# Two of four mean subtractions in each layer norm given to GpSimd, with a third difference buffer

## The chip, the cores and the metric

The kernel runs on one core of a Trainium2 chip. A core has five engines with queues of their own: TensorE (PE in the profile: matmuls, and PEld for its weight loads), VectorE (DVE), ScalarE (ACT), GpSimd (POOL) and SyncE (SP, which here only starts DMAs). Every engine works through its queue strictly in order and waits on semaphores for the others. The metric is the time of one execution on the device in microseconds (us).

## The reference

The input x has 2048 rows of 1024 features, in bfloat16. Four blocks follow one another, A, B, A, B, each with a residual:

```python
def _layernorm(x, axis=-1, eps=1e-5):
    m = jnp.mean(x, axis=axis, keepdims=True)
    v = jnp.var(x, axis=axis, keepdims=True)
    return (x - m) / jnp.sqrt(v + eps)
...
x = x + _A_ref(_layernorm(x, axis=-1), A_wqkv, A_w_phi, A_wo)
x = x + _B_ref(_layernorm(x, axis=-1), B_wqkv, B_wo)
x = x + _A_ref(_layernorm(x, axis=-1), A_wqkv, A_w_phi, A_wo)
x = x + _B_ref(_layernorm(x, axis=-1), B_wqkv, B_wo)
```

A is linear attention with 32 heads of 32: queries and keys go through a small projection w_phi, and two softmaxes over 32 features (of the value and of its negative) make the feature maps. B is softmax attention with 32 heads over all 2048 rows. The change touches only the subtraction x - m.

## The kernel before

The residual x stays in SBUF, transposed: xT has the 1024 features as 8 groups of 128 partitions, and the 2048 rows lie along the free dimension, in four chunks c of 512. A "layer" is one A block with the B block after it. In layer 0, A's keys and values are made chunk by chunk (`a_keys`, L651), then the queries and the output of A chunk by chunk (`a_queries`, `a_out`), and behind each chunk the layer norm of B for it, then B's keys and values; after that comes B's attention. Its scores are matmuls at L1049, three 128x512 blocks to one exponential on ScalarE (L1095); a number of the blocks go to VectorE instead (L1171 and L1013). The sums over keys are the matmuls of L1199. While layer 0's attention runs, its layer norms and keys for layer 1's A block are made beside it for three of the chunks (`alone=True`). Layer 1 makes those of the fourth chunk by itself, then goes on as layer 0 does.

`layernorm` (L524) for one chunk:
- squares of x on ScalarE (L536; on VectorE at L541 when alone), and two groups of eight matmuls with a matrix of 1/1024 (through `mmgroup`, recorded at L480) that give mean and mean square in every partition
- mean squared and a copy of the mean to SBUF on ScalarE (L556, L558); the variance on VectorE (L559, one input in PSUM, one in SBUF); log and exponential on ScalarE (L561, L563) give the reciprocal deviation
- for i = 0 to 3, each two feature groups, 128 x 1024 elements: the subtraction s_i (L569: x in bfloat16 minus the mean, into a float32 buffer of the class "lnw") and the multiplication m_i (L573: that buffer times the reciprocal deviation, into bfloat16). The matmuls of keys, queries or values take the four parts one after the other.

There are 16 such layer norms: three are alone, inside the attention of layer 0, and 13 are not: 4 for A and 4 for B in layer 0, 1 for A and 4 for B in layer 1. I call them A0 to A3 and B0 to B3 by their chunk.

The order on every engine is made by a planner in the kernel, `Sched`. Each operation is entered with its engine, an assumed duration, what it depends on, its buffers and a priority (`op`, L61). `run` (L173) then plays this through: at each assumed moment every free engine takes its ready operation with the lowest priority number whose buffers can be had. Buffers come from one arena of 162 KB per partition; `QUOTA` (L305) says how many of a class may live at once, and "lnw" has 2. The result is a fixed order for each engine's queue. So any assumed duration or quota that changes moves instructions on all engines. VectorE's share of the exponentials is also settled there (`attach`, L1131, with the limits in `MOST`), and so are filler matmuls for moments in which the plan leaves TensorE idle (L1423, L1418).

Of GpSimd, the kernel before asks for a few constants, two memsets of 128x2048 (L744) and 64 small copies of 128x32 in `a_keys` (L689), which put the sums of the feature maps beside the values.

Of the kernel before, what the change touches and what calls it, by code (L numbers as in the profile page):

```python
# [48 lines left out]
class Sched:  # L49
# [11 lines left out]
    def op(self, eng, dur, fn, deps=(), bufs=(), prio=0.0, lat=None, mode=None):  # L61
        o = Op(eng, dur, LAT[eng] if lat is None else lat, fn, tuple(bufs), prio, mode, len(self.ops))
        for d in deps:
            if d is not None:
                d.out.append(o)
                o.ndep += 1
        for b in o.bufs:
            b.left += 1
        self.ops.append(o)
        return o  # L70
# [102 lines left out]
    def run(self):  # L173
# [27 lines left out]
        while left:  # L201
# [102 lines left out]
MODEST = {"slabk", "xn1", "e1", "vp1", "pkf", "lnw1", "w2o", "bo"}  # L304
QUOTA = {"pk": 3, "pv": 2, "kv": 1, "ln": 2, "mm": 2, "cmp": 2, "bc": 4, "num": 1, "wt": 4, "fil": 2,  # L305
         "e": 6, "vp": 6, "e1": 4, "vp1": 4, "E": 6, "q2": 3, "kt": 3, "w2": 5, "w2o": 3, "oT": 26, "T": 4, "den": 2,
         "lnt": 6, "lnw": 2, "lnw1": 1, "eq": 8, "ns": 4, "cw": 6, "hl": 6, "oc": 2, "slab": 7, "slabk": 3, "fin": 4,
         "rs": 8, "pkf": 1, "cden": 2, "part": 8, "w2r": 1,
         "xs": 1, "xy": 2, "xx": 1, "E1": 6}
SPELL = 3.4  # L310
# [4 lines left out]
EXP2_B, EXP2_C, EXP2_R = -0.9409531310034907, 6.912204565299476, 0.8383392207797716  # L315
LAG = 5
AHEAD = 36
SLACK = 8.0
NEAR = 20
LEAD = 3.0  # L320
# [3 lines left out]
def act_us(n):  # L324
    return n / 1200 + 0.064


def dve_us(n):
    return n / 960 + 0.15
# [6 lines left out]
def kernel(  # L336
# [11 lines left out]
    nc = tc.nc  # L348
# [35 lines left out]
    hl = const.tile([P, 1], F32, tag="hl")  # L384
# [49 lines left out]
    op = sch.op  # L434

    def sb(cls, *dims, dt=BF16):
        n = 1
        for d in dims:
            n *= d
        b = Buf("sb", -(-n * (4 if dt == F32 else 2) // 64) * 64, cls)  # L440
        b.with_ = ()

        def v():
            ap = arena[:, b.at // 2:b.at // 2 + n * (2 if dt == F32 else 1)]
            if dt == F32:
                ap = ap.bitcast(F32)
            if len(dims) == 2:
                ap = ap.rearrange("p (a b) -> p a b", a=dims[0])
            elif len(dims) == 3:
                ap = ap.rearrange("p (a b c) -> p a b c", a=dims[0], b=dims[1])  # L450
            return ap

        return b, v

    def ps(cls, banks):
        b = Buf("ps", 0, cls, banks)

        def v():
            return psum[:, b.at[0] * C512:(b.at[-1] + 1) * C512]

        return b, v
# [9 lines left out]
    def csl(c):  # L471
        return slice(c * C512, (c + 1) * C512)
# [20 lines left out]
    def mmgroup(pb, pv, lhs, rhs, deps, pdeps, bufs, prio, n=PO):  # L493

        last = None
        cols, us, mode = kind(pb)
        for i in range(n // 2):
            def fn(i=i):
                for po in (2 * i, 2 * i + 1):
                    mm(pv(), lhs(po), rhs(po), po == 0, po == n - 1, cols)  # L500
            last = op(
                "PE", 2 * us, fn, flat([last, deps if i == 0 else (), pdeps[i] if pdeps else None]),
                [pb, *bufs], prio, mode=mode,
            )
        return last
# [15 lines left out]
    def deps_x(c):  # L521
        return list(xdone[c])

    def layernorm(c, prio, banks, alone=False, n=2):  # L524

        xb, xv = sb("xn1" if alone else "xn", PO, C512)
        t_b, t_v = sb("lnt", C512, dt=F32)
        m_b, m_v = sb("lnt", C512, dt=F32)
        r_b, r_v = sb("lnt", C512, dt=F32)
        halves = []  # L530
        parts = [deps_x(c)[2 * i:2 * i + 2] for i in range(4)]
        for h in range(n):
            hs = slice(8 // n * h, 8 // n * h + 8 // n)
            if not alone:
                halves.append(op(
                    "ACT", act_us(4096 // n), lambda hs=hs: nc.scalar.activation(  # L536
                        out=xv()[:, hs, :], in_=xT[:, hs, csl(c)], func=ACT.Square),
                    parts[h] if n == 4 else deps_x(c), [xb], prio))
            else:
                halves.append(op(  # L540
                    "DVE", 2048 / 1920 + 0.15, lambda hs=hs: nc.vector.tensor_tensor(  # L541
                        out=xv()[:, hs, :], in0=xT[:, hs, csl(c)], in1=xT[:, hs, csl(c)], op=ALU.mult),
                    deps_x(c), [xb], prio))
        mb, mv = ps("fil" if alone else "ln", banks)
        qb, qv = ps("fil" if alone else "ln", banks)
        if not alone:
            mb.with_ = (qb,)
        m = mmgroup(mb, mv, lambda po: onesD[:], lambda po: xT[:, po, csl(c)], (), parts if n == 4 else [deps_x(c)] * 4, [], prio)
        q = mmgroup(qb, qv, lambda po: onesD[:], lambda po: xv()[:, po, :], [m],
                    halves if n == 4 else [halves[0], None, halves[1], None], [xb], prio + 0.01)  # L550
        if alone:
            mc = op("DVE", dve_us(512), lambda: nc.vector.tensor_copy(out=m_v(), in_=mv()), [m], [mb, m_b], prio)
            msq = op("DVE", dve_us(512), lambda: nc.vector.tensor_tensor(
                out=t_v(), in0=m_v(), in1=m_v(), op=ALU.mult), [mc], [m_b, t_b], prio)
        else:
            msq = op("ACT", act_us(512), lambda: nc.scalar.activation(out=t_v(), in_=mv(), func=ACT.Square),  # L556
                     [m], [mb, t_b], prio)
            mc = op("ACT", act_us(512), lambda: nc.scalar.copy(out=m_v(), in_=mv()), [m], [mb, m_b], prio)  # L558
        var = op("DVE", dve_us(512), lambda: nc.vector.tensor_tensor(  # L559
            out=t_v(), in0=qv(), in1=t_v(), op=ALU.subtract), [q, msq], [qb, t_b], prio)  # L560
        ln = op("ACT", act_us(512) + 0.1, lambda: nc.scalar.activation(  # L561
            out=t_v(), in_=t_v(), func=ACT.Ln, bias=eps[:, 0:1]), [var], [t_b], prio)
        rstd = op("ACT", act_us(512), lambda: nc.scalar.activation(  # L563
            out=r_v(), in_=t_v(), func=ACT.Exp, scale=-0.5), [ln], [t_b, r_b], prio)
        fin = []
        for i in range(4):
            pr = slice(2 * i, 2 * i + 2)
            w_b, w_v = sb("lnw1" if alone else "lnw", 2, C512, dt=F32)
            s1 = op("DVE", dve_us(1024), lambda pr=pr, w_v=w_v: nc.vector.tensor_tensor(  # L569
                out=w_v(), in0=xT[:, pr, csl(c)],  # L570
                in1=m_v().unsqueeze(1).to_broadcast([P, 2, C512]), op=ALU.subtract),
                [mc, *deps_x(c)], [m_b, w_b], prio)
            fin.append(op("DVE", dve_us(1024), lambda pr=pr, w_v=w_v: nc.vector.tensor_tensor(  # L573
                out=xv()[:, pr, :], in0=w_v(),
                in1=r_v().unsqueeze(1).to_broadcast([P, 2, C512]), op=ALU.mult),
                [s1, rstd, q], [r_b, w_b, xb], prio))
        return xb, xv, fin
# [447 lines left out]
    def attention(base, kT, vT, q_of, gate, most):  # L1025
# [13 lines left out]
        def prio_of(u):  # L1039
            qc, g, pp, d, j = u  # L1040
            return base + 10 * pos[(qc, g)] + 5 * pp + 0.5 * d
# [76 lines left out]
        def wants(prio):  # L1118
            at = state["at"] + AHEAD + 8
            if at > len(units):  # L1120
                return False
            u = units[state["at"]]
            turn = pos[u[:2]]
            if prio < prio_of(u) + SLACK:
                return False
            if state["pair"] is None and (state["turn"].get(turn, 0) + 2 > most(turn)
                                          or sch.live.get("xy", 0) >= QUOTA["xy"] or sch.live.get("E1", 0) >= QUOTA["E1"]):
                return False
            return all(d.done == 2 for d in needs(units[at - 1]))

        def attach(so, grp, extra):  # L1131
# [3 lines left out]
            turn = pos[grp[0][:2]]  # L1135
            end = state["at"] + AHEAD + 8 > len(units)
            if end or pair is not None and index[pair["units"][0]] < state["at"] + NEAR:
                close(pair)
                pair = None
            if end or (pair is None and state["turn"].get(turn, 0) + 2 > most(turn)):  # L1140
                return
            u = next((u for u in units[state["at"] + AHEAD:state["at"] + AHEAD + 8]
                      if u[4] in rows and u not in taken
# [144 lines left out]
    for layer in range(2):  # L1288
# [13 lines left out]
        for c in chunks:  # L1302
            xnA[c] = layernorm(c, base + 10 * c - 9 if base + c else -16.0, ANY, n=4 if layer else 2)
            a_keys(c, base + 10 * c, wk_s, wv_s, kv, ANY)
# [23 lines left out]
        for c in range(NC):  # L1328
            pr = second + 20 * c
            o_b, o_v = sb("oc", G, C512)  # L1330
            oc = (o_b, o_v, {})
# [12 lines left out]
        for g in range(1, G):  # L1344
            pr = at + 10 * pos[(0, g)] - 19
# [8 lines left out]
        for g in range(G):  # L1354
            pr = at + 10 * pos[(0, g)]
# [31 lines left out]
        for i in range(G):  # L1387
            pr = p0 - 7 + 2 * i
# [9 lines left out]
        for i in range(G):  # L1398
            pr = p0 + 20 + i
# [7 lines left out]
        if not last:  # L1407

            kv = new_kv()
            for c, p0 in ((0, 190), (1, 220), (2, 265)):  # L1410
                xb, xv, fin = xnA[c] = layernorm(c, at + p0, FIL, True)
# [47 lines left out]
```

## Time and profile before

| | us |
|---|---|
| three runs, median | 2438.75 |
| lowest and highest of them | 2437.62, 2442.32 |
| the profiled execution: its own time | 2438.97 |
| its span, first to last instruction | 2437.2 |
| busy in the span: PE, ACT | 2270.0, 2084.6 |
| busy in the span: DVE, POOL | 1553.0, 26.0 |
| L569, 64 subtractions on DVE | 78.0, 1220 ns each |
| L573, 64 multiplications on DVE | medians of 1225 ns |
| L689, 64 copies on POOL | 21.8, median of 326 ns |

The spans of the stages, read from the timeline: loads and the first layer norm to about 60 us, keys and values of A to 190, queries, output and B's norms to 375, attention with the keys for layer 1 to 1310, the A block of layer 1 to 1560, attention to the end.

How to read it: a group row in the profile names line, engine and operation, what is written from what, the shape, the count, then busy time and mean length, then the time in which the engine stood idle before it and for whom. Two instructions on VectorE overlap a little in the records, so back to back ones start 1.14 us apart though each lasts 1.22. The page's chain is the sequence of work that ended last, followed backwards from the end.

### The profile page before, as it was taken

The page shows a single profiled execution, that of the slowest core. Times are in us where ns is not written, and L with a number is a line of the kernel's source. Part 1 is how long each engine was busy: PE and PEld are TensorE (multiplying, and loading weights), DVE is VectorE, ACT ScalarE, POOL GpSimd, SP SyncE. Part 2 cuts the span into 40 slices and gives each one's busy share as a digit, 9 for nine tenths or more (in the row PEclk, how much of TensorE's full clock was granted, in tenths as well). Part 3 has the DMA queues.
Part 4 walks back from the last instruction along what each step waited for, and adds up shares of the span by engine and source line. Part 5 has one row for each costly group of instructions (what it writes and reads, how often), then busy time and mean ns, then how long its engine had stood idle before and what let it go on. Part 6 is the DMA issues. An engine that isn't in the chain of part 4 may idle for free.

```text
span 2437.2 us, 62702 instructions
## 1 busy us (share of the span) xinstructions
PE 2270.0 (93%) x27608; PEld 881.5 (36%) x27608; DVE 1553.0 (64%) x2212; ACT 2084.6 (86%) x1856; POOL 26.0 (1%) x72
## 2 busy tenths in 40 slices
PE   7999999999999999999899999999999999999998
PEld 4443443333333333333333444343333333333333
DVE  6997663343568766544646766323477887687885
ACT  6325648999999999999996555689999999999997
POOL 0000000000000000000000000000000000000000
PEclk9999999999999999999999999999999999999999
DMA  9020011111212121213414001011111121111000
GB/s 220 21 64 1 5 35 27 39 37 44 60 48 67 48 64 54 91 42 93 119 62 129 11 5 36 18 32 35 39 44 39 33 68 35 39 32 33 20 20 33
DMA packets 216411, 118.41 MB, mean 49 GB/s; under 512 B 138568, under 2 KB 206152, under 8 KB 215368
## 3 DMA queue, kind: packets, MB, share of 16 engines
q1 hardware_dynamic: 215080, 112.29, 17.1%
q8 instruction: 216, 3.54, 0.6%
q10 hardware_dynamic: 1056, 2.10, 0.2%
q14 instruction: 59, 0.48, 0.1%
HBM read 78.71 MB, written 14.14 MB: 38 GB/s over the span
## 4 chain that ended last, share of the span: by engine, by line
ACT 50%; PE 27%; issue 10%; DVE 9%; DMA 2%; SPq 1%; ACTq 0%; POOL 0%; DVEq 0%
ACT arena L1095 47%; PE psum L480 14%; PE psum L484 5%; PE psum L1049 3%; PE psum L1199 3%; ACT arena L671 1%; DVE arena L675 1%; SPq L515 1%; DVE arena L573 1%; DVE arena L569 1%; PE psum L839 1%; DVE work L1013 1%; DMA arena<-arena 1%; DVE arena L684 1%; ACT arena L536 1%
## 5 line engine op out<-in xcount | busy, mean ns | idle before, releaser
L1095 ACT ACTIVATE arena<-psum 128x1536 bf16<-128x1536 f32 x1301 | 1755.3, 1669 | 33.7 <-PE psum L1049 32.0
L1199 PE MATMUL psum<-arena 128*32 128x512 bf16 x4096 | 620.6, 384 | 4.4 <-DVE arena L1214 4.4
L1199 PE MATMUL psum<-arena,ones_bf 128*32 128x512 bf16 x4096 | 620.7, 384 | 0.0
L1049 PE MATMUL psum<-arena 32*128 32x512 bf16 x4096 | 511.9, 383 | 101.6 <-ACT arena L1095 93.5
L484 PE MATMUL psum<-arena 128*32 128x512 bf16 (+1 forms) x8768 | 578.1, 375 | 7.8 <-DVE arena L668 2.4
L480 PE MATMUL psum<-arena 128*128 128x512 bf16 (+1 forms) x2032 | 462.1, 376 | 22.2 <-DVE arena L573 6.0
L1049 PEld LDWEIGHTS <-arena 32*128 32x128 bf16 x4096 | 176.3, 91 | 620.1 <-issue 608.7
L480 PEld LDWEIGHTS <-arena 128*128 128x128 bf16 x2032 | 193.2, 98 | 259.6 <-issue 55.9
L484 PEld LDWEIGHTS <-arena 128*32 128x32 bf16 x8768 | 199.3, 96 | 233.7 <-issue 113.0
L1199 PEld LDWEIGHTS <-arena 128*32 128x32 bf16 x4096 | 162.3, 95 | 230.9 <-issue 173.7
L1013 DVE SCALAR_TENSOR_TENSOR work<-work 128x1024 f32<-128x1024 f32 (+1 forms) x222 | 240.7, 1084 | 4.7
L898 DVE CAST arena<-psum 128x512 bf16<-128x512 f32 (+1 forms) x128 | 84.1, 657 | 247.0 <-PE psum L484 243.0
L1171 DVE TENSOR_SCALAR work<-psum 128x512 int32<-128x512 f32 x194 | 133.5, 688 | 86.1 <-PE psum L1049 85.2
L1199 PEld LDWEIGHTS <-ones_bf 128*32 128x32 bf16 x4096 | 160.9, 95 | 22.7 <-issue 5.3
L1013 DVE SCALAR_TENSOR_TENSOR arena<-work 128x1024 bf16<-128x1024 f32 (+1 forms) x111 | 120.6, 1087 | 2.9
L671 ACT ACTIVATE arena<-psum 128x512 bf16<-128x512 f32 x80 | 42.8, 600 | 85.2 <-PE psum L480 56.1
L801 ACT ACTIVATE arena<-psum 128x512 bf16<-128x512 f32 x128 | 69.8, 597 | 40.6 <-PE psum L480 31.9
L1214 DVE COPY arena<-psum 128x512 f32<-128x512 f32 x126 | 86.3, 685 | 25.9 <-PE psum L1199 24.4
L675 DVE TENSOR_REDUCE arena<-arena 128x32 f32<-128x1024 bf16 x64 | 77.8, 1215 | 36.5 <-ACT arena L671 34.7
L1423 PE MATMUL psum<-xT,zero 128*32 128x512 bf16 x1296 | 100.1, 381 | 0.0
L569 DVE TENSOR_TENSOR arena<-xT,arena 128x1024 f32<-128x1024 bf16 x64 | 78.0, 1220 | 34.0 <-ACT arena L558 32.2
L1255 DVE TENSOR_TENSOR arena<-arena 64x512 bf16<-64x512 f32 x124 | 84.7, 683 | 14.6 <-DMA arena<-rd 10.0
(97 smaller groups left out, 1424.9 us busy)
## 6 DMA issues: line engine op xcount, KB each, us to landing
arena<-rd SPq DMA_DIRECT2D x62, 256.0 KB
arena<-in_B_wqkv_dram SPq DMA_DIRECT2D x48, 256.0 KB
arena<-in_A_wqkv_dram SPq DMA_DIRECT2D x10, 1024.0 KB
arena<-arena SPq DMA_DIRECT2D x256, 32.0 KB
arena<-in_B_wo_dram SPq DMA_DIRECT2D x32, 256.0 KB
arena<-wd_k SPq DMA_DIRECT2D x8, 1024.0 KB
arena<-arena SPq DMA_DIRECT2D x96, 64.0 KB
arena<-in_A_wo_dram SPq DMA_DIRECT2D x4, 1024.0 KB
```

Of the source, the lines that this page charges most:

```text
L480: nc.tensor.matmul(out_, lhsT=lhsT, rhs=rhs, start=start, stop=stop, skip_group_check=True)
L484: nc.tensor.matmul(out_[ks, :], lhsT=lhsT[:, ks], rhs=rhs, start=start, stop=stop, tile_position=(0, 32 * k), skip_group_check=True)
L569: s1 = op("DVE", dve_us(1024), lambda pr=pr, w_v=w_v: nc.vector.tensor_tensor(out=w_v(), in0=xT[:, pr, csl(c)], in1=m_v().unsqueeze(1).to_ ...
L675: red = op("DVE", dve_us(1024), lambda ev=ev, sv=sv: nc.vector.reduce_sum(out=sv(), in_=ev().rearrange("p s (h d) -> p (s h) d", d=DH), ax ...
L1013: return sch.later("DVE", dve_us(n * 512), lambda: nc.vector.scalar_tensor_tensor(out=out_(), in0=in0(), scalar=scalar, in1=in1(), op0=ALU ...
L1049: nc.tensor.matmul(out=out_, lhsT=kT[g][1]()[r, pp, d * P:(d + 1) * P], rhs=q_of[(qc, g)][1]()[r, (pp + j // 2) % 2, :], start=True, stop= ...
L1095: ex = make("ACT", act_us(w * C512), lambda: nc.scalar.activation(out=e_v()[:, 0:w * C512], in_=s_v(), func=ACT.Exp, scale=e_scale), [so], ...
L1171: pair["got"].append(sch.later("DVE", dve_us(512), lambda: nc.vector.tensor_scalar(out=y_v().bitcast(I32)[:, k, :], in0=s_v(), scalar1=EXP ...
L1199: nc.tensor.matmul(out=a_v()[col:col + 32, :], lhsT=v_v()[:, kc % 4, o:o + DH] if what == 0 else ones_bf[:], rhs=ev()[:, x * C512:(x + 1) ...
L1214: cp = op("DVE", dve_us(512), lambda t_v=t_v, a_v=a_v: nc.vector.tensor_copy(out=t_v(), in_=a_v()), [last], [a_b, t_b], prio - 4)
L1255: s = [op("DVE", dve_us(512), lambda a=a, k=k, o_v=o_v, r_v=r_v, T=T: nc.vector.tensor_tensor(out=o_v()[a, :], in0=T[k][1]()[a, :], in1=r_ ...
L1423: nc.tensor.matmul(psum[32 * k:32 * k + 32, 6 * C512:7 * C512], lhsT=zero[:], rhs=xT[:, 0, 0:C512], start=False, stop=False, tile_position ...
```

## The change

In the layer norms that are not alone, s_1 and s_3 are issued on GpSimd, and entered in the plan with 2.8 us; s_0 and s_2 stay on VectorE, and so do all four multiplications. The quota of "lnw" goes from 2 to 3, 4 KB per partition more while all three live.

```diff
-         "lnt": 6, "lnw": 2, "lnw1": 1, "eq": 8, "ns": 4, "cw": 6, "hl": 6, "oc": 2, "slab": 7, "slabk": 3, "fin": 4,
+         "lnt": 6, "lnw": 3, "lnw1": 1, "eq": 8, "ns": 4, "cw": 6, "hl": 6, "oc": 2, "slab": 7, "slabk": 3, "fin": 4,
...
+GP = (1, 3)
...
             w_b, w_v = sb("lnw1" if alone else "lnw", 2, C512, dt=F32)
-            s1 = op("DVE", dve_us(1024), lambda pr=pr, w_v=w_v: nc.vector.tensor_tensor(
+            eng, us = (nc.gpsimd, 2.8) if not alone and i in GP else (nc.vector, dve_us(1024))
+            s1 = op("POOL" if eng is nc.gpsimd else "DVE", us, lambda pr=pr, w_v=w_v, eng=eng: eng.tensor_tensor(
                 out=w_v(), in0=xT[:, pr, csl(c)],
                 in1=m_v().unsqueeze(1).to_broadcast([P, 2, C512]), op=ALU.subtract),
                 [mc, *deps_x(c)], [m_b, w_b], prio)
```

## The prediction

> **What bounds the kernel now.** I began with the busy time of each engine in stretches of the span (columns: PE, PEld, DVE, ACT, POOL, each busy us with its count, then granted clock, DMA share, GB/s):
>
> ```profile
> 60.00:120.00 60.00, 55.82 (x364) 28.64 (x362) 57.99 (x90) 19.83 (x37) 2.92 (x9) 1.00 0.05 16
> 120.00:180.00 60.00, 57.50 (x328) 28.19 (x326) 55.63 (x83) 17.42 (x33) 4.55 (x14) 1.00 0.26 75
> ...
> 300.00:360.00 60.00, 59.88 (x313) 24.88 (x312) 38.18 (x55) 31.72 (x51) 0.00 (x0) 1.00 0.14 36
> 480.00:540.00 60.00, 57.64 (x819) 20.58 (x820) 27.54 (x47) 60.00 (x46) 0.00 (x0) 1.00 0.15 39
> 1500.00:1560.00 60.00, 51.55 (x327) 22.21 (x326) 32.38 (x38) 30.14 (x41) 0.00 (x0) 0.91 0.06 14
> ```
>
> Four regimes: while A's keys are made (60 to 159) VectorE has no gap; while queries are made (300 row) TensorE is full; in attention (480 row) ScalarE is; and near 1500 none is, so a chain of waits counts. The timeline of VectorE in that last stretch shows the chain, norm B3 of layer 1:
>
> ```profile
> 1543.60 1.23 DVE L569 TENSOR_TENSOR arena<-xT,arena 128x1024 f32<-128x1024 bf16 x1 [3.15 <-ACT arena L558]
> 1544.75 0.69 DVE L559 TENSOR_TENSOR arena<-psum,arena 128x512 f32<-128x512 f32 x1
> 1545.35 1.22 DVE L569 TENSOR_TENSOR arena<-xT,arena 128x1024 f32<-128x1024 bf16 x1
> 1546.88 2.36 DVE L573 TENSOR_TENSOR arena<-arena 128x1024 bf16<-128x1024 f32 x2 [0.32 <-ACT arena L563]
> ```
>
> Two buffers let s0 and s1 run before the reciprocal deviation is there; then m0, m1, s2, m2, s3, m3 follow, 7.2 us (1546.88 to 1554.05), all of them in the chain that ended last. The same pass lies in the chain at 378.23 (B3, layer 0) and 1503.81 (B2, layer 1); A3 of layer 1 (1320.56) is in it in part. Last, GpSimd beside VectorE (timeline, both engines):
>
> ```profile
> 936.72 1.21 DVE L1013 SCALAR_TENSOR_TENSOR arena<-work 128x1024 bf16<-128x1024 f32 x1
> 936.83 1.29 POOL L689 CAST arena<-arena 128x32 bf16<-128x32 f32 x1 [749.75 <-DVE arena L668]
> ```
>
> This decides most of what follows. 63 of the 64 casts last 0.32 to 0.33 us, and those run beside VectorE instructions that read one SBUF input (L684 and L721 read PSUM and SBUF) or none (L668). This one alone meets an instruction with two SBUF inputs, and it ends 0.19 us after that instruction (936.72 + 1.21 = 937.93; 936.83 + 1.29 = 938.12). GpSimd was **held** while VectorE read two SBUF operands. L569 and L573 are of that kind, and so is the moved subtraction.
>
> The Trainium skill, "SBUF — State Buffer", section "Who interferes with whom", states it both ways: a VectorE instruction with two SBUF inputs and a GpSimd instruction that reads SBUF exclude each other, and whichever starts first holds the other for its whole length. The trace agrees in one direction, by the 1.29 us above; the other no row of before shows.
>
> **What moves.** In the order of instructions as built, 26 subtractions of 128x1024 leave VectorE (64 to 38) and stand on GpSimd: two for each of 13 norms. Beside that the plan comes out new on every engine.
>
> **The price of one on GpSimd** is not in the trace. Its memset writes 128x2048 in 1.84 us, 0.92 for 1024 elements of one stream; a small cast costs 0.33. With its two reads and one write all overlapped I get 0.92 + 0.33 = 1.25 us, one after the other 3 x 0.92 + 0.33 = 3.1, with the two reads in turn and the write beside them 2.2. I take 2.2, the middle way, and keep 1.25 and 3.1 for the range.
>
> The Trainium skill, "GPSIMD Engine Reference", section "Performance versus the Vector engine", measures 4497 ns for 2048 elements; half, 2.25, would be an estimate by that page, and the sum below would rise by under 1 us.
>
> **Keys of A, 60 to 159.** VectorE loses s1 and s3 of A1, A2, A3: 6 x 1.15 (start to start) = 6.9 us. Against it stand the holds, in the built order, 2.3 us each with the handover, less what VectorE does meanwhile with instructions that read one SBUF input:
> - A1's s1: the mean is there at 63.21 and s0 started at 63.45, VectorE being busy till then. GpSimd starts 0.16 after what it waits for (reciprocal ends 62.21, cast starts 62.37), so at 63.37, ahead of s0: 2.2 lost (0.7 if s0 is first, then s2 waits).
> - A1's s3 starts after m0, beside four copies of L718 (1.06): m1 waits 1.3. A2's s1 is next in GpSimd's queue, again beside four copies: m2 waits 1.3.
> - A2's s3: m1 follows m0 at once and goes first; then four adds of L721 (1.06) stand ahead of m2: 1.2. A3's s1, beside L684 (1.23): 1.2. A3's s3, beside L684, L559 and L721: 0.
>
> Sum 7.2, so +0.3 net (-1.2 with the shorter A1). Without holds the gain is not 6.9 but at most what TensorE has idle in 60 to 180, 120 - 55.82 - 57.50 = 6.7: say -6. The small casts queued behind a subtraction on GpSimd are not late: L703 needs the first of them only some 10 us later (A2's first at 80.82, L703 at 90.57). A0's norm lies under the load of x (to 40.8), as the chain there runs through SP and DMA.
>
> **Norms under TensorE's queries** (B0 to B2 of layer 0, B0 and B1 of layer 1): TensorE is full (59.88 of 60), and the built order puts as much of its work or more between the statistics and the first use as before. I count 0; uncovered, each would cost what the next part gives.
>
> **Exposed norms** (B3 of layer 0; A3, B2, B3 of layer 1). VectorE idles for the mean, starts 0.03 after it and so beats GpSimd's 0.16. B3, layer 1: s0 to 1544.83, s1 on GpSimd to 1547.1, and s2, the third buffer's, is held till then and ends at 1548.35; so m0 starts 1.5 later than 1546.88. Likewise A3: +1.5; B3 of layer 0 (mean 374.23, m0 378.23): +0.8; B2 (mean 1498.61, m0 1503.81): 0. Then m0 to m3 take 3 x 1.15 + 1.24 = 4.7, and s3 needs its own 2.2 and two handovers (0.3), since any multiplication beside it is held or holds it: 7.2, as before. Sum +3.8. Without holds: m0 on time, m1 and m2 under s3, so 1.15 + 0.16 + 2.2 + 0.1 + 1.24 = 4.9 instead of 7.2, four times -2.3 = -9.2. The built order counts on that: TensorE has about 4 fillers fewer (0.43 us each) ahead of the later parts of these norms, up to 1.7 more each that I leave to the range.
>
> **Attention.** The new plan gives VectorE 202 score blocks instead of 194. ScalarE's exponentials go from 639 to 637 in layer 1; in layer 0 one of 662 becomes 1024 columns narrower. At 810.9 / 603 = 1.345 us each (1600 to 2430, ScalarE busy 811.6 of 830): -2.7, and 1.345 - 0.48 for a 512-wide one: -0.85. VectorE has room (576.6 of 830). Together -3.5; other shifts in these 1800 us I bound by 4 either way.
>
> **Sum**, against the profiled execution's own 2438.97 (span 2437.2, 1.8 around it, 0.2 over the median): +0.3 + 3.8 - 3.5 = +0.6, so 2439.6, and 2439.4 against the median. I say **2439.5**: no change that can be told (0.2% is 4.9 us, about what a measurement of this kernel can tell).
>
> **The rivals.**
> - *No hold while GpSimd reads*: -6 - 9.2 - 3.5 = -18.7, 2420. For it: nothing in before shows VectorE held, and the hold of GpSimd is one event. Against it: that event is clean, 1.29 beside 63 of 0.33. Chance 0.2.
> - *Slower: a GpSimd subtraction takes 3.1.* Each of the five held ones among A's keys costs 0.9 more, 4.5; in the exposed norms s1 puts m0 later by 0.9 three times and by 0.55 for B2, and s3 adds 4 x 0.9: 6.9. In all +12: 2451. It decides from 2.5 us: 12.7 us per us of length, and 4 us are missing to 0.2%. For it: the diff itself enters 2.8, and three streams in turn give 3.1. Chance 0.25.
> - *The new plan outweighs the edit*: fillers and scores shift by more than I bound, either sign, 2430 or 2448; 0.1.
> - That nothing moves is excluded: the built order has the 26.
>
> **How the numbers follow.** The forecast has 0.45 and its own range, 2435 to 2446: 0.02 faster, 0.33 same, 0.10 slower. No hold adds 0.19 faster, 0.01 same; the long subtraction 0.25 slower; the new plan 0.04, 0.04, 0.02. Faster 0.25, same 0.38, slower 0.37. The range goes from 2423 (half of the no-hold case left out) to 2451 (half of the slow one).
>
> **What would show it.** Subtractions of 2.2 us on GpSimd, some longer where a multiplication was first; s2 and m1 or m2 on VectorE longer than 1.22, to 2 or 3 us, beside them; the pass from m0 to m3 at 7.2 in B3, not 4.9; m0 about 1 to 1.5 later after the mean; VectorE still without a gap from 60 to 159 and A's keys ending within 1 us of before; 637 exponentials in layer 1. Multiplications of 1.22 throughout would prove me wrong, as would a GpSimd row far from 2.2.

## The result and the profile after

The changed kernel takes 2447.66 us (median of six runs, 2443.82 to 2449.53) against 2438.64 before: 1.0034 of it, 95% interval 1.0021 to 1.0047. It is **slower by 9.0 us**. That lies in the range on record and outside the forecast's own (2435 to 2446): of the signs I gave, "slower" held 0.37, "no change" 0.38. The profiled execution after took 2443.82 (span 2442.0), the fastest of its six; 4.85 of the 9.0 us can be placed in its trace.

The stretches that were shown of before, now after (PE, PEld, DVE, ACT, POOL, clock, DMA share, GB/s):

```profile
60.00:120.00 60.00, 54.19 (x354) 28.20 (x359) 57.76 (x87) 19.74 (x37) 13.66 (x14) 1.00 0.02 8
120.00:180.00 60.00, 57.74 (x329) 28.46 (x333) 55.41 (x84) 17.66 (x34) 8.52 (x16) 1.00 0.26 76
...
1500.00:1560.00 60.00, 53.20 (x308) 24.92 (x312) 35.03 (x42) 28.24 (x43) 9.36 (x3) 0.97 0.04 9
```

Six subtractions have left VectorE in the first two rows, and it is as busy as before (57.76 and 55.41 against 57.99 and 55.63). The groups of the page, and the subtractions left on VectorE, say why (count, busy us, mean ns):

```profile
L575 DVE TENSOR_TENSOR arena<-arena 128x1024 bf16<-128x1024 f32 x64 | 97.1, 1556 | 3.2 <-ACT arena L564 2.6
...
L571 POOL TENSOR_TENSOR arena<-xT,arena 128x1024 f32<-128x1024 bf16 x26 | 76.3, 2936 | 442.0 <-ACT arena L559 411.4
```

```profile
L571 DVE TENSOR_TENSOR arena<-xT,arena 128x1024 f32<-128x1024 bf16 x38 | 58.1, 1530 | 36.7 <-ACT arena L559 35.5 <-PE psum L705 0.9 <-PE psum L1201 0.2
```

Lines are one or two numbers later than before (573 is 575). On average multiplications went from 1224 to 1556 ns, and the 38 subtractions that stay on VectorE from 1220 to 1530. That is 64 x 0.33 + 38 x 0.31 = 33 us of holds on VectorE, for 26 x 1.22 = 32 us taken off it. The move gave VectorE no time back.

How one hold looks, in norm B3 of layer 1, first VectorE's timeline, then GpSimd's:

```profile
1556.02 1.22 DVE L571 TENSOR_TENSOR arena<-xT,arena 128x1024 f32<-128x1024 bf16 x1 [3.15 <-ACT arena L559]
1557.17 0.68 DVE L560 TENSOR_TENSOR arena<-psum,arena 128x512 f32<-128x512 f32 x1
1557.77 2.57 DVE L571 TENSOR_TENSOR arena<-xT,arena 128x1024 f32<-128x1024 bf16 x1
1560.26 6.56 DVE L575 TENSOR_TENSOR arena<-arena 128x1024 bf16<-128x1024 f32 x4
```

```profile
1556.12 3.13 POOL L571 TENSOR_TENSOR arena<-xT,arena 128x1024 f32<-128x1024 bf16 x1 [32.16 <-ACT arena L559]
1561.55 3.05 POOL L571 TENSOR_TENSOR arena<-xT,arena 128x1024 f32<-128x1024 bf16 x1 [2.30 <-DVE arena L575]
```

VectorE's s0 starts 0.10 ahead and holds GpSimd's s1 to 1557.25; then s1 reads for 2.0 us, to 1559.25, and holds s2, whose record of 2.57 contains that wait. The variance (L560, one input in PSUM) passes unhindered. Then m0, m1, m2, m3 take 6.56 instead of four times 1.15, as s3 came between m1 and m2.

The stages of the two profiled executions, lengths in us. Ends are read from the timeline: the last reduction of A's keys, the last add of A's output for chunk 0, the starts of the 51st, 401st and 701st exponential and of layer 0's last log (L1231 before), the last instruction.

| stage | before | after | difference | forecast |
|---|---|---|---|---|
| to the end of A's keys, layer 0 | 186.2 | 185.9 | -0.3 | +0.3 |
| first chunk of queries and output | 47.6 | 51.9 | +4.3 | 0 |
| other chunks, B0 to B3, to the 51st exponential | 217.6 | 218.7 | +1.1 | +0.8 |
| to the 401st exponential | 472.4 | 471.7 | -0.7 | |
| to the end of layer 0's attention | 383.5 | 391.5 | +8.0 | -0.85 with the row above |
| layer 1: A3, queries, B0 to B3, to the 701st | 294.8 | 295.3 | +0.5 | +3.0 |
| the rest of layer 1's attention | 835.1 | 827.0 | -8.1 | -2.7 |
| sum | 2437.2 | 2442.0 | +4.8 | +0.6 |

### The profile page after: what moved, and what is told of

Read it like the earlier page. It is cut to its first block, busy times and chain, and to the rows that moved or that the text cites. A ratio compares the mean times of both kernels' runs of the same rounds, so it can differ in the third digit from the quotient of the medians.

```text
span 2442.0 us, 62295 instructions
## 1 busy us (share of the span) xinstructions
PE 2257.2 (92%) x27359; PEld 880.4 (36%) x27424; DVE 1578.0 (65%) x2219; ACT 2080.3 (85%) x1854; POOL 101.0 (4%) x98
## 4 chain that ended last, share of the span: by engine, by line
ACT 26%; PE 13%; DVE 6%; issue 5%; DMA 0%; ACTq 0%; SPq 0%; DVEq 0%
ACT arena L1097 24%; PE psum L481 5%; PE psum L485 3%; PE psum L1201 2%; PE psum L1051 2%; DVE arena L575 1%; DVE work L1015 1%; DVE arena L571 1%; ACT arena L537 0%; PE psum L841 0%; DVE work L1173 0%; DVE arena L1257 0%; DVE work L1017 0%; DVE arena L677 0%; DVE work L1020 0%
## 5 line engine op out<-in xcount | busy, mean ns | idle before, releaser
L1201 PE MATMUL psum<-arena 128*32 128x512 bf16 x4096 | 618.8, 384 | 11.2 <-DVE arena L1216 10.2
L1201 PE MATMUL psum<-arena,ones_bf 128*32 128x512 bf16 x4096 | 618.8, 384 | 0.0
L481 PE MATMUL psum<-arena 128*128 128x512 bf16 (+1 forms) x1977 | 455.2, 375 | 29.4 <-DVE arena L575 12.9
L1015 DVE SCALAR_TENSOR_TENSOR work<-work 128x1024 f32<-128x1024 f32 (+1 forms) x232 | 251.1, 1083 | 5.3
L1201 PEld LDWEIGHTS <-arena 128*32 128x32 bf16 x4096 | 163.5, 95 | 234.1 <-issue 176.0
L1173 DVE TENSOR_SCALAR work<-psum 128x512 int32<-128x512 f32 x202 | 139.0, 688 | 87.1 <-PE psum L1051 85.5
L1201 PEld LDWEIGHTS <-ones_bf 128*32 128x32 bf16 x4096 | 161.8, 95 | 28.8 <-issue 11.1
L1015 DVE SCALAR_TENSOR_TENSOR arena<-work 128x1024 bf16<-128x1024 f32 (+1 forms) x116 | 125.5, 1082 | 3.0
L575 DVE TENSOR_TENSOR arena<-arena 128x1024 bf16<-128x1024 f32 x64 | 97.1, 1556 | 3.2 <-ACT arena L564 2.6
L1257 DVE TENSOR_TENSOR arena<-arena 64x512 bf16<-64x512 f32 x124 | 84.7, 683 | 18.2 <-DMA arena<-rd 11.1
L571 POOL TENSOR_TENSOR arena<-xT,arena 128x1024 f32<-128x1024 bf16 x26 | 76.3, 2936 | 442.0 <-ACT arena L559 411.4
```

Of the source, the lines that this page charges most:

```text
L481: nc.tensor.matmul(out_, lhsT=lhsT, rhs=rhs, start=start, stop=stop, skip_group_check=True)
L571: s1 = op("POOL" if eng is nc.gpsimd else "DVE", us, lambda pr=pr, w_v=w_v, eng=eng: eng.tensor_tensor(out=w_v(), in0=xT[:, pr, csl(c)], i ...
L1015: return sch.later("DVE", dve_us(n * 512), lambda: nc.vector.scalar_tensor_tensor(out=out_(), in0=in0(), scalar=scalar, in1=in1(), op0=ALU ...
L1173: pair["got"].append(sch.later("DVE", dve_us(512), lambda: nc.vector.tensor_scalar(out=y_v().bitcast(I32)[:, k, :], in0=s_v(), scalar1=EXP ...
L1201: nc.tensor.matmul(out=a_v()[col:col + 32, :], lhsT=v_v()[:, kc % 4, o:o + DH] if what == 0 else ones_bf[:], rhs=ev()[:, x * C512:(x + 1) ...
L1257: s = [op("DVE", dve_us(512), lambda a=a, k=k, o_v=o_v, r_v=r_v, T=T: nc.vector.tensor_tensor(out=o_v()[a, :], in0=T[k][1]()[a, :], in1=r_ ...
```

## The experiments

Two theories were tried. **Holds**: GpSimd and VectorE exclude each other while both read SBUF, and that takes back what VectorE was relieved of. **Plan**: the planner's new order of all engines costs the time, whoever does the subtractions. Times are medians of 5 to 11 runs; ratios are against before's runs on the same chip, with a 95% interval.

**The new plan with the work on VectorE** (e1_plan_only):

```diff
-            s1 = op("POOL" if eng is nc.gpsimd else "DVE", us, lambda pr=pr, w_v=w_v, eng=eng: eng.tensor_tensor(
+            s1 = op("POOL" if eng is nc.gpsimd else "DVE", us, lambda pr=pr, w_v=w_v: nc.vector.tensor_tensor(
```

> The plan of the changed kernel, instruction for instruction (202 score blocks on VectorE, 1299 exponentials), but s1 and s3 are issued on VectorE at the same place in the order; GpSimd has its small casts alone, so nothing is held. Theory holds (the slowdown comes from GpSimd and VectorE holding each other): back to 2436 to 2441. Theory plan (the slowdown comes from the new order of all engines): stays near the changed kernel, 2445 to 2450, with the stall of ScalarE at 1118 to 1126 and the later end of layer 0's attention still there. If both share, 2441 to 2445.

2447.23, ratio 1.0031 (1.0019 to 1.0044). By its face this is for the plan. It isn't decisive: this order was made for a VectorE without s1 and s3, and here it had to do them too.

**The new plan with GpSimd only writing but for a small cast** (e2_write_only, and e9_write_only_long with the second memset):

```diff
+            def blank(w_v=w_v):
+                nc.gpsimd.tensor_copy(out=w_v()[:, 0, 0:8], in_=m_v()[:, 0:8])
+                nc.gpsimd.memset(w_v(), 0.0)
+                nc.gpsimd.memset(w_v(), 0.0)
```

> The changed kernel and its plan, but in place of each subtraction GpSimd makes a cast of 8 columns of the mean and a memset of the difference buffer: about the same length (0.33 + 1.8 us), the same wait for the mean, but hardly a read of SBUF. s1 and s3 are left out of the computation. Theory holds: multiplications of 1.22 throughout, the pass from m0 to m3 near 5 us, A's keys some 6 us earlier than before; 2430 to 2438. Theory plan: the layer norms get shorter in the same way, but the stalls of the attention stay; 2438 to 2445. Theory that GpSimd's writes hold VectorE too: 2446 to 2450, with multiplications of 2 to 3 us as in the changed kernel.

> The plan of the changed kernel, and in place of each subtraction a cast of 8 columns and two memsets instead of one. The first write-only run had memsets of 0.95 us, so its GpSimd work was some 1.3 us where a subtraction takes 2.14; with two it is 0.33 + 2 x 0.95 = 2.2. s1 and s3 are left out of the computation. Theory holds: near the shorter one, 2429 to 2433, as the 0.9 us more are hidden beside VectorE's work except before m3. If the gain of the first one came from its shorter GpSimd work: 2438 or more.

2429.38, ratio 0.9964 (0.9951 to 0.9978), and with the length mended 2428.46, ratio 0.9966 (0.9953 to 0.9978). Both lie within 1 us under the bands of the holds theory. So it is not the length, and GpSimd's memsets hold nothing. The groups of the longer one:

```profile
L580 DVE TENSOR_TENSOR arena<-arena 128x1024 bf16<-128x1024 f32 x64 | 76.2, 1222 | 14.8 <-POOL arena L575 7.1 <-ACT arena L564 7.0
L576 DVE TENSOR_TENSOR arena<-xT,arena 128x1024 f32<-128x1024 bf16 x38 | 46.3, 1221 | 36.9 <-ACT arena L559 35.4 <-PE psum L710 0.9 <-PE psum L1206 0.2
L574 POOL MEMSET arena<- 128x1024 f32 x26 | 24.7, 951 | 3.6 <-issue 2.1
```

VectorE is back at 1.22 throughout, in the same order. The small cast, which does read SBUF, lasts 0.19 us in 5 of 26 cases and 1.12 to 1.25 in the other 21: it is held by VectorE as the cast of 1.29 was in the profile before, and no row of VectorE shows a hold by it. With that a step takes GpSimd 2.9 us on average (1.0 + 2 x 0.95), about as long as the subtraction with its waits, 2.94; the 2.2 in the expectation left the wait out. What GpSimd reads costs 2447.66 - 2428.46 = 19.2 us in this plan, or 17.9 when each is taken against the before that was measured with it (2438.64 and 2437.36). The Trainium skill, "SBUF — State Buffer", section "Who interferes with whom", says that a GpSimd instruction that only writes does not contend with two SBUF inputs on VectorE; these rows agree.

**The third buffer alone, and two nudges of the plan** (e3_third_buffer has quota 3 and all subtractions on VectorE; e4_plan_nudge and e8_plan_nudge_less are the kernel before with another assumed length):

```diff
-GP = (1, 3)
+GP = ()
...
-            s1 = op("DVE", dve_us(1024), lambda pr=pr, w_v=w_v: nc.vector.tensor_tensor(
+            s1 = op("DVE", dve_us(1024) + 0.02, lambda pr=pr, w_v=w_v: nc.vector.tensor_tensor(
```

> Quota 3 for the difference buffer alone, all subtractions on VectorE (191 score blocks there, 1302 exponentials). VectorE does the same work as before. Theory holds: no change, 2436 to 2441. Theory plan: the third buffer moves the order too, so it may go either way by up to 5 us, 2434 to 2444.

> The kernel before, with 0.02 us more entered in the plan for each subtraction outside attention; every instruction stays on its engine, only the order changes (201 score blocks on VectorE, 1299 exponentials). Theory holds: 2436 to 2441, and less with two exponentials fewer. Theory plan: it shows how far a new order alone moves the time; 3 us or more either way would say that the 9 us of the change can be of that kind, under 2 us that they can't.

> The kernel before with 0.02 us less entered in the plan for each subtraction outside attention (194 score blocks, 1301 exponentials); only the order changes. Theory plan: another draw of what a new order costs; three so far were +7.6, +8.3 and +16.5, so 2442 to 2457. If +0.02 was a special case, within 3 us of before.

2446.49, ratio 1.0031 (1.0019 to 1.0042); 2455.42, 1.0070 (1.0057 to 1.0082); 2444.31, 1.0028 (1.0016 to 1.0039). The first lies above both of its bands. No subtraction changed its engine in any of the three, and 0.02 us in the plan's arithmetic costs 5.8 us when taken off and 16.5 when added. More than the order moves: in the kernel with 0.02 added, as in the changed one, the planner also moved some score blocks to VectorE (201 instead of 194). A new plan alone can move this kernel as far as the whole change did, so no comparison of two plans can tell what the move is worth. Where the move itself is judged from here on, the order is kept.

**The old plan with the work on GpSimd, and with GpSimd only writing** (e5_old_plan_gpsimd, e6_old_plan_write_only; planned as VectorE's, issued elsewhere, two buffers; the second uses the cast and one memset from above):

```diff
+            eng = nc.gpsimd if not alone and i in (1, 3) else nc.vector
-            s1 = op("DVE", dve_us(1024), lambda pr=pr, w_v=w_v: nc.vector.tensor_tensor(
+            s1 = op("DVE", dve_us(1024), lambda pr=pr, w_v=w_v, eng=eng: eng.tensor_tensor(
```

> The order of the kernel before, unchanged on every engine, with two buffers, but s1 and s3 of the norms outside attention are issued on GpSimd at their place in it. It is the move without the new plan. Theory holds cancel the move: 2436 to 2444 (in the new plan the move was worth 2447.7 - 2447.2 = +0.4), with GpSimd rows of 2.1 to 3.2 us and multiplications of up to 3.2. With two buffers s2 and s3 wait longer, so the upper end is likelier. If the move by itself costs: 2445 or more, as the changed kernel.

> As the run beside it, with the order of before, but GpSimd makes a cast of 8 columns of the mean and a memset instead of each subtraction; s1 and s3 are left out of the computation. Theory holds: without them the move is worth about what it was in the new plan, 2429.4 - 2447.2 = -17.8, or less as two buffers leave s2 behind m0: 2421 to 2432. If the gain there came from how the new plan lays things out: 2434 or more.

2446.51, ratio 1.0036 (1.0024 to 1.0049), and 2428.64, ratio 0.9963 (0.9950 to 0.9975). In before's own order the move alone costs 7.9 us, more than the holds theory had put in its band (2436 to 2444), and with GpSimd only writing it gains 9.9. Of the first:

```profile
L574 DVE TENSOR_TENSOR arena<-arena 128x1024 bf16<-128x1024 f32 x64 | 97.0, 1543 | 23.4 <-ACT arena L563 20.1 <-POOL arena L570 2.2
L570 POOL TENSOR_TENSOR arena<-xT,arena 128x1024 f32<-128x1024 bf16 x26 | 72.1, 2776 | 439.9 <-ACT arena L558 398.3 <-PE psum L480 16.9 <-PE psum L704 14.1
L570 DVE TENSOR_TENSOR arena<-xT,arena 128x1024 f32<-128x1024 bf16 x38 | 48.7, 1282 | 33.9 <-ACT arena L558 32.2 <-PE psum L484 1.3
```

The same holds are there, now mostly on the multiplications, as s2 comes later with two buffers.

**No hold, with the whole computation** (e7_psum_operands): the reciprocal deviation goes into a PSUM bank, and VectorE takes the mean from PSUM.

```diff
+        if not alone:
+            r_b, r_v = qb, qv
         rstd = op("ACT", act_us(512), lambda: nc.scalar.activation(
...
+            a_b, a_v, ad = (m_b, m_v, mc) if alone or eng is nc.gpsimd else (mb, mv, m)
...
-                in1=m_v().unsqueeze(1).to_broadcast([P, 2, C512]), op=ALU.subtract),
-                [mc, *deps_x(c)], [m_b, w_b], prio)
+                in1=a_v().unsqueeze(1).to_broadcast([P, 2, C512]), op=ALU.subtract),
+                [ad, *deps_x(c)], [a_b, w_b], prio)
```

> The changed kernel with the whole computation, made free of holds: the reciprocal deviation is written to the PSUM bank of the mean square instead of SBUF, and s0 and s2 read the mean from its PSUM bank, so that VectorE's subtractions and multiplications have one SBUF input each; s1 and s3 stay on GpSimd. The banks live longer, and the plan comes out new (194 score blocks, 1301 exponentials). Theory holds: GpSimd rows of 2.14, no multiplication above 1.3, and some 18 us under the same order with holds; as the plan is new again, its own shift (+7.6, +8.3 and +16.5 in three plans so far) is added to 2421 to 2430: 2421 to 2440. If PSUM operands don't free the two engines: rows of 3 us again, and 2440 to 2455.

2435.7, ratio 0.9991 (0.9982 to 0.9999): the fastest kernel here that computes everything, if only by 0.1% and with an interval that nearly reaches no change. The groups, and B3 of layer 1:

```profile
L578 DVE TENSOR_TENSOR arena<-arena,psum 128x1024 bf16<-128x1024 f32 x52 | 61.1, 1217 | 16.2 <-ACT psum L566 15.6
L574 POOL TENSOR_TENSOR arena<-xT,arena 128x1024 f32<-128x1024 bf16 x26 | 55.7, 2146 | 441.7 <-ACT arena L559 404.5 <-DVE arena L578 32.4 <-PE psum L481 4.8
```

```profile
1546.22 4.76 DVE L578 TENSOR_TENSOR arena<-arena,psum 128x1024 bf16<-128x1024 f32 x4 [2.11 <-ACT psum L566]
```

GpSimd's subtraction is 2.15 us, every one of 26 between 2139 and 2159 ns, and the pass from m0 to m3 takes 4.76 with s3 beside it. As its plan is its own, two controls kept that order exactly: the reciprocal deviation in SBUF again (e10_psum_plan_held), and s1 and s3 on VectorE (e12_psum_plan_vector).

```diff
+            r_b = qb
+            r_v = lambda k=len(norms) % 3: work[:, k, 0:C512]
+            norms.append(c)
...
-            s1 = op("POOL" if eng is nc.gpsimd else "DVE", us, lambda pr=pr, w_v=w_v, eng=eng, a_v=a_v: eng.tensor_tensor(
+            s1 = op("POOL" if eng is nc.gpsimd else "DVE", us, lambda pr=pr, w_v=w_v, a_v=a_v: nc.vector.tensor_tensor(
```

> The kernel with PSUM operands, its order the same instruction for instruction, but the reciprocal deviation is written to a fixed place in SBUF, so the multiplications have two SBUF inputs again; the mean of s0 and s2 stays in PSUM. The whole computation. Theory holds: multiplications of 2 to 3.2 us beside GpSimd rows of 2.1 to 3.1, and 2435.7 plus 5 to 13 (of 18 in the changed kernel's plan, without those that s2 met): 2441 to 2449. If PSUM operands did nothing and only their plan was lucky: 2434 to 2438.

> The kernel with PSUM operands, its order the same instruction for instruction, but s1 and s3 are issued on VectorE at their place. The whole computation. In the changed kernel's plan and in the one before, taking GpSimd's work off VectorE without holds was worth 17.8 and 9.9 (both with the shorter writes in place of subtractions). So 2435.7 plus 8 to 18: 2443 to 2454. If GpSimd gives nothing even without holds: 2434 to 2438.

2448.0, ratio 1.0044 (1.0032 to 1.0057), and 2453.49, ratio 1.0072 (1.0059 to 1.0084). One operand's place is worth 12.3 us, or 13.5 with each taken against before on its own chip (2438.56 and 2437.36), and the rows show it as holds:

```profile
L582 DVE TENSOR_TENSOR arena<-arena,work 128x1024 bf16<-128x1024 f32 x52 | 81.3, 1613 | 16.2 <-ACT work L570 16.0
...
L578 POOL TENSOR_TENSOR arena<-xT,arena 128x1024 f32<-128x1024 bf16 x26 | 65.2, 2509 | 442.3 <-ACT arena L561 404.8 <-DVE arena L582 29.8 <-PE psum L481 4.8
```

**A truer length in the plan** (e11_psum_own_length: 2.14 for 2.8 in the kernel with PSUM operands):

> The kernel with PSUM operands and 2.14 us entered for GpSimd's subtraction instead of 2.8, its measured length without a hold (195 score blocks, 1301 exponentials). The plan is new once more. Theory plan: a draw from the same spread, 2428 to 2445; a plan that knows the true length should wait for GpSimd less, which gives the lower half, and at best a kernel below 2435.

2441.06, ratio 1.0015 (1.0006 to 1.0024): within its band, but not in the lower half that was expected, and 5.4 slower than with 2.8. The plan that knew the length was not the better one.

Three orders, three ways (us):

| order of | s1, s3 on VectorE | on GpSimd, held | on GpSimd, not held |
|---|---|---|---|
| the kernel before | 2438.6 | 2446.5 | 2428.6, only writes |
| the changed kernel | 2447.2 | 2447.7 | 2428.5, only writes |
| the kernel with PSUM operands | 2453.5 | 2448.0 | 2435.7, whole computation |

Along each row the order is fixed: the instructions of every engine stand in the same sequence in the traces, the moved ones aside (65 of the changed kernel's matmul records are missing). By these medians holds cost 17.9, 19.2 and 12.3; against before on each kernel's own chip, 17.9, 17.9 and 13.5. The profiled executions show where. The held kernel's stages, less those of the one without holds (us):

| order of | A's keys, layer 0 | B0 to B3, layer 0 | A3, queries, B0 to B3, layer 1 | whole span |
|---|---|---|---|---|
| the kernel before (e5 less e6) | 6.5 | 3.2 | 8.0 | 17.6 |
| the changed kernel (after less e9) | 3.1 | 3.1 | 8.8 | 14.2 |
| the kernel with PSUM operands (e10 less e7) | 3.4 | 1.8 | 9.1 | 14.2 |

In all three orders the cost lies in the stages that have the norms, and the other stages together come to less than 1 us. **That reads on GpSimd and two SBUF inputs on VectorE hold each other, and that this takes back what the move relieves, is shown.** One reserve stands: in the write-only kernels GpSimd's large inputs are gone, and zeros are computed with in their place, and in before's order only the shorter write was tried; the pair e7 and e10 alone has the whole computation.

How much of the 9.0 us is the move and how much the plan is not shown, for it depends on which is changed first. With the move first (by e5) the move is 7.9 and the plan 1.2; with the plan first (by e1) the plan is 8.6 and the move 0.4. For work split as in the change, the new plan is about as good as before's (1.2 and -0.1 apart in the two columns with GpSimd); with all subtractions on VectorE it is 8.6 worse, as it was made for a lighter VectorE.

## Why the prediction was right and wrong, by its steps

**The hold** was read rightly from one cast of 1.29 us, and it works both ways, where before could show one direction only: VectorE's s2 above is 2.57, GpSimd's s1 3.13. **The price** of 2.2 is 2.14 where nothing holds it; the rows of 2.99 to 3.19 contain a wait of some 1 us for VectorE. The size came from a choice between three ways of adding up streams, and no run shows that the two reads come in turn; there luck had a part.

**A's keys**: forecast +0.3, in the trace -0.3, and that is luck. The kernels in the same order take it apart. A1's first subtraction starts at 63.45 before and at 65.75 to 66.55 in all four kernels of the new order, held or not; the sum had no term for that. From there to the end of A's keys it takes 122.8 us before, 123.6 in e1, 116.7 in e9 and 120.2 in the changed kernel. So the relief was the 6.9 of the forecast, the holds took back 3.5 where I had 7.2, and the new order cost some 3. There were as many holds as I had counted, but shorter ones. One case came out otherwise: in A1, VectorE's s0 (65.75) beat GpSimd's s1 (65.85), the shorter of my two cases. The next ones are there, here m1 and then m2 with m3, held by s3 of A1 and s1 of A2 in a row, for 0.95 and 0.87 where I put 1.3 each:

```profile
72.32 2.17 DVE L575 TENSOR_TENSOR arena<-arena 128x1024 bf16<-128x1024 f32 x1
74.52 0.93 DVE L720 COPY arena<-psum 32x66 f32<-32x66 f32 x4
75.48 3.23 DVE L575 TENSOR_TENSOR arena<-arena 128x1024 bf16<-128x1024 f32 x2
```

**Exposed norms**: forecast +3.8 in four; the two stage rows have +1.1 and +0.5. In B3 of layer 1 the mean to m0 takes 4.27 (1555.99 to 1560.26) instead of 3.31, +1.0 where I put +1.5, and m0 to m3 takes 6.56 where I put 7.2. The held s2 ends 1.09 us after its release (1559.25 to 1560.34), not 1.22 and a handover, as if its start lay under the wait. So the length of a hold was oversized by some 0.3 us each.

**Hold against no hold**: I put 2439.5 - 2420 = 19 us between my forecast and the rival; the runs have 17.9 to 19.2. The difference came out, but both ends were too low by some 8 us (2447.7 and 2428.5). In before's order, where the plan has no part, what was mis-sized is the relief: -6 for A's keys and -9.2 for the norms, without holds, against 9.9 for all. Its A keys (e6) end only 2.1 us earlier (184.1), and there VectorE waits 5.5 us for ScalarE's exponentials instead of 2.1: the next thing late was not TensorE's idle 6.7, as I assumed, but the chain through ScalarE. In layer 1's norms the relief was 5.8 of my 6.9, in layer 0's stage with B3 it was 0.3 of 2.3.

**Attention and the new plan**: this is the step that failed. "Together -3.5; other shifts in these 1800 us I bound by 4 either way." Layer 0's attention took 7.3 more (-0.7 and +8.0), layer 1's 8.1 less, and the first queries, put at 0, 4.3 more. Together these stages have +3.5 where the sum had -3.5, while keys and norms have +1.3 where it had +4.1; the two errors make the 4.2 between +0.6 and +4.8. The shifts belong to the order: e1 and e9 have them too (first queries 51.5 and 53.6, end of layer 0's attention 393.0 and 390.8, rest of layer 1's 826.7 and 827.0), and the kernels in before's order don't (e5 48.0, 382.5, 832.3). One stall of the +8.0, in the timeline of all engines:

```profile
1121.71 1.41 DVE L1257 TENSOR_TENSOR arena<-arena 64x512 bf16<-64x512 f32 x2 [4.02 <-DMA arena<-rd]
...
1123.93 0.69 DVE L1216 COPY arena<-psum 128x512 f32<-128x512 f32 x1
...
1124.68 0.38 PE L1201 MATMUL psum<-arena 128*32 128x512 bf16 x1 [3.34 <-DVE arena L1216]
...
1126.28 1.45 ACT L1097 ACTIVATE arena<-psum 128x1536 bf16<-128x1536 f32 x1 [2.70 <-PE psum L1201]
```

The new order puts a scaling that needs a DMA ahead of the copy that frees TensorE's accumulator: VectorE waits 4.02 for the DMA, TensorE 3.34 for VectorE, ScalarE 2.70 for TensorE. In that stretch ScalarE's waits for L1201 go from 0.2 to

```profile
ACT arena L1097 <- PE psum L1201: 8.1, 4, 2.7
```

I had costed the plan by its counts of instructions (202 blocks, two exponentials fewer) and not by what stands ahead of what. The two fewer are there, in layer 1's -8.1; the rest of that is the idle time of ScalarE, 11.1 before and 5.6 after. Some 2.8 of the -8.1 is not the order's: e5 and e6, with before's order, took 832.3 and 832.1 there, and of these three only the profile of before has a spell of lower clock in that stage (0.72 from 1960 to 1966).

**From the trace to the median**, 4.2 us: the profiled execution after is the fastest of its kernel, that of before 0.3 above its median. Among the six runs the time goes with the granted clock (2443.82 at 0.995, 2446.13 at 0.993, 2447.5 and 2447.8 at 0.992, 2448.9 and 2449.5 at 0.991). The lower clock goes with the new order, whoever subtracts: on one chip e1 has 0.990 to 0.994 and e2 0.992 to 0.995, before 0.993 to 0.997, e5 and e6, in before's order, 0.995 to 0.999. In the trace one spell of it (0.66 from 1124 to 1129) comes right behind TensorE's wait of 3.34 us that is shown above. Whether such waits are the cause is not shown.

**The rivals**: "no hold" described the write-only kernels well in kind, at 8 us too good. "Slower by 3.1 us a subtraction" named the right sign with a wrong cause: the subtraction isn't longer, the wait in its record is. "The new plan outweighs the edit", at 0.1, had about the right size for e1 and e3 (its 2448 against 2447.2 and 2446.5), too much for e8 and too little for e4, and should have had more weight.

## What to carry to other kernels

In this kernel work on GpSimd that reads SBUF relieved VectorE only where the VectorE instructions beside it read at most one operand from SBUF. So count those that read two first, and move an operand to PSUM (here worth 12.3 us) or give GpSimd work that only writes. Where a planner lays out the whole kernel, test an edit inside a fixed order and draw a few plans beside it; here a nudge of 0.02 us moved the time by 5.8 and 16.5 us. Read a GpSimd row together with VectorE's at the same moment, since both records contain the wait for the other.

## What the runs showed of the hardware beside that

- GpSimd takes its turn between two back to back VectorE instructions that have nothing to wait for: s3 of B3 in layer 1 came between m1 and m2, with no gap in VectorE's queue. In ten of the 13 norms one multiplication is longer by 1.93 to 1.95 us in this way.
- GpSimd's memset costs by the element, not the byte, in these two forms: 0.95 us for 128x1024 in float32, 1.84 for 128x2048 in bfloat16.
- A multiplication with one operand in PSUM takes VectorE 1217 ns, with both in SBUF 1224.
- Runs of one kernel spread over 9 us with the granted clock: among those of before on one chip, from 2433.8 at 0.998 to 2442.9 at 0.992.
